# Folding the keys into wq with two half-width column tiles, and 64 bytes ahead of the left-hand tiles

## The chip, the core and the metric

The kernel runs on one core of a Trainium2 chip. The time is the device time of one execution in microseconds; where several runs are shown, their median. Beside the times there is the profile of one execution, with the instructions of every engine, the DMA queues and the TensorE clock that was granted.

## What is computed

Two operators read the same x (2048 tokens of 576 values, float32), and a gate mixes them token by token:

```
g   = sigmoid(sum(x * gate_w))
a   = irfft2(rfft2(x) * (w_r + i w_i))
q   = x @ w_q                       # 32 heads, two halves of 128
s1  = q[..., :128] @ k1.T           # 64 keys;  s2 = q[..., 128:] @ k2.T
e   = 64 * argmax(s1) + argmax(s2)  # one expert of 4096 per token and head
b   = sum over heads of gelu(x . u[e]) * v[e]
out = g * a + (1 - g) * b
```

With one expert per head the softmax over the chosen scores is 1. The table of experts has u and v side by side, so one row is 1,152 float32 values, 4,608 bytes.

## The kernel before, in words

**The keys are folded into w_q.** q itself is never built. For each chunk c of 4 heads (8 chunks) and each block i of the model dimension (four of 128 rows and a last one of 64) the kernel computes M = w_q · k, so that the scores are x · M. That is `build_m` (L442), called 40 times. `load_wq` (L399) brings a block of w_q into a tile of the ring uv, as 8 groups g of 128 columns: 4 heads times two halves. Even g belong to k1, odd g to k2. `kTb` holds the keys, negated, as three blocks of 64 columns: k1, k2, k1. For each g there is one fp32 product: the 128 columns of w_q's group are the stationary operand, and 128 key columns from `half * 64` on are moved. So each product yields 128 columns in PSUM, 64 of the keys wanted and 64 of the other ones. Only the first 64 are read afterwards (`pv()[:, :, :E]` with E = 64). ScalarE copies them as `mh` rounded to the matmul type fp32r (L459), and a remainder `ml` is made: on VectorE in chunk 0 (L468), later by an identity product that subtracts `mh` in PSUM (`less`, L461) and a copy on ScalarE. One call of the fp32 product stands in the profile as two matmuls (passes), each with a weight load of its own.

**Scores.** `scores` (L474) multiplies, for two tiles of 128 tokens at a time, x and its remainder (tiles `xt`) with `mh` and `ml` into PSUM tiles of 1,024 scores, of which there are four. VectorE takes the maximum over each group of 64 (L504); ScalarE makes the signs of the difference to it (L512); VectorE reduces these to an index (L528 to L542), which ScalarE writes out as an expert's number.

**Gathers and their use.** `group` (L631) gathers, for token tiles 0 to 9, one row of 4,608 bytes per token and head from HBM (L638, issued by GpSimd, 128 rows each) into one of the 12 buffers of the ring uv. VectorE forms x · u (L650), ScalarE the gelu, and the v halves are added up in three ways: VectorE alone (L682), ScalarE scaling and VectorE adding (L675, L676), or TensorE with a diagonal matrix (L706). For the token tiles 10 to 15 `quad` (L738) does the same later, with gathers at L745, dots at L754 and TensorE products that use 32 of the array's columns for each of four heads (L766).

**The transform** comes behind the scores: `fold` (L892), then units of `f2`, `f4`, `f5`, `f6`, then `invert` (L1066). `fold` and `f6` use array tiles of 32 columns too. The gathers of `quad` run beside it.

**The order** of the work is a list written out by hand, RANK, one place for each job of the planner (`Plan`, L108), which runs them through a model of the engines and fixes the order on every engine. `mm` (L347) and `on` chain each engine's instructions in that order. A set of products is planned at 1.74 us (`plan("PE", 1.74, ...)`).

**Memory.** Tiles are allocated in pools from the left (pp, sm, gp, then sp, and lb in its place later) and from the right (pad, xp, sa, later la). `pad` is 96 bytes on the right, cleared by a memset at L288. gp holds the 12 buffers of uv and kT, among others; sp holds the tiles `mh`, `ml` and some of `xt`; the tiles with an x at the end of their names (`mhx`, `mlx`) lie in sa, on the right.

The products before:

```
for g in range(8):
    half = g % 2
    mm(
        pv()[:, g, :], wq.ap[:, g, :],
        kTb.ap[:, half * 64 : half * 64 + 128], start=g % 4 == 0, stop=g % 4 == 3, skip_group_check=True)
```

Of the kernel before, what the change touches and what calls it, by code (L numbers as in the profile page):

```python
# [12 lines left out]
F32 = mybir.dt.float32  # L13
# [7 lines left out]
P = 128  # L21
# [7 lines left out]
E = 64  # L29
# [228 lines left out]
def dve(n, psum=False):  # L258
    return 0.07 + n / 960


def act(n):
    return 0.1 + n / 1250
# [15 lines left out]
def tile_kernel(ctx, tc, xn, xT, x5, wqT, wq5, kT, wri, uv, gw, t_kr, t_ff, t_fv, t_tw, t_io, out):  # L279
    nc = tc.nc  # L280
    PS = bass.MemoryType.PSUM

    pools = {}
    pools["pp"] = ctx.enter_context(tc.tile_pool(name="pp", bufs=1))
    pools["sm"] = ctx.enter_context(tc.tile_pool(name="sm", bufs=2))
    pools["gp"] = ctx.enter_context(tc.tile_pool(name="gp", bufs=1))
    pad = ctx.enter_context(tc.tile_pool(name="pad", bufs=1, side="right"))
    nc.vector.memset(pad.tile([P, 24], F32, tag="pad", name="pad"), 0.0)  # L288
    pools["xp"] = ctx.enter_context(tc.tile_pool(name="xp", bufs=1, side="right"))
# [7 lines left out]
    def after(chain, i):  # L297
        if chain in prev:
            tc.add_manual_dep(
                i.ins, prev[chain].ins.name,  # L300
                mybir.DependencyInfo(mybir.DependencyClass.NoSync, mybir.DependencyReason.DATA),
                reason="order of the work")
        prev[chain] = i
# [26 lines left out]
    def buf(tag, shape, dt=F32, view=None):  # L330
        ids[0] += 1
        name = f"{tag if isinstance(tag, str) else tag[0]}_{ids[0]}"

        def make(g, slot):
            p, n = home[g]
            x = pools[p].tile(shape, dt, tag=f"{g}.{slot}", bufs=1, name=name)
            return view(x) if view else x

        return Buf((tag,) if isinstance(tag, str) else tag, make)

    def psum():
        return buf("p2", [P, 2, 512])

    def nd(*k):
        return NUDGE.get(k, 0.0)

    def mm(*args, **kw):  # L347
        after("PE", nc.tensor.matmul(*args, **kw))  # L348
# [8 lines left out]
    def dv(us, at, fn, w, r, **kw):  # L357
        return plan("DVE", us, at, lambda: on("DVE", fn()), w, r, **kw)

    def ac(us, at, fn, w, r, **kw):  # L360
        return plan("ACT", us, at, lambda: on("ACT", fn()), w, r, **kw)
# [30 lines left out]
    kTb = buf("kT", [P, 192])  # L392
# [49 lines left out]
    def build_m(c, i, at, after=()):  # L442
        at = at + nd("b", c, i)
        mh, ml = m_t[c, i] = [
            buf(n + "x" if c % 2 == 0 and i < MX else n, [P, CW], F32R) for n in ("mh", "ml")]
        pm = psum()
        wq = wq_t[c, i]
        pv = lambda: pm.ap.rearrange("p a (g e) -> p (a g) e", e=128)

        def go():  # L450
            for g in range(8):
                half = g % 2
                mm(
                    pv()[:, g, :], wq.ap[:, g, :],
                    kTb.ap[:, half * 64 : half * 64 + 128], start=g % 4 == 0, stop=g % 4 == 3, skip_group_check=True)

        plan("PE", 1.74, at, go, [pm], [wq, kTb], after=after)
        v3 = lambda m: m.ap.rearrange("p (g e) -> p g e", e=E)
        ac(act(512), at + O_MH, lambda: actv(v3(mh), pv()[:, :, :E], AF.Copy, scale=-1.0), [mh], [pm])  # L459
        if c >= LOW_PE:  # L460
            def less():  # L461
                for r in range(2):
                    mm(pv()[:, 4 * r : 4 * r + 4, :E], ident, v3(mh)[:, 4 * r : 4 * r + 4, :], start=False, stop=True, skip_group_check=True)

            plan("PE", 0.25, at + O_LESS, less, [pm], [mh, "ident"])
            ac(act(512), at + O_ML, lambda: actv(v3(ml), pv()[:, :, :E], AF.Copy, scale=-1.0), [ml], [pm])
            return
        dv(dve(512, True), at + O_ML, lambda: stt(v3(ml), pv()[:, :, :E], -1.0, v3(mh).bitcast(F32), op0=ALU.mult, op1=ALU.subtract), [ml], [pm, mh])  # L468
# [964 lines left out]
```

## Time and profile before

| what | value |
|---|---|
| median of 3 runs | 944.68 us (942.21 to 947.41) |
| profiled execution | 953.06 us, span 951.3 us |
| granted TensorE clock, mean | 0.963 |
| products on kT (one of the page's groups) | 640 matmuls, 81.0 us busy |
| gathers: L638 and L745 | 320 and 192, 128 rows each |
| HBM traffic over the span | 362 GB/s |

The profiled execution is one execution and not among the three timed ones. PE is TensorE's matmuls and PEld its weight loads, which run beside them; DVE is VectorE, ACT ScalarE, POOL GpSimd and SP the queue of the plain loads. The tile form 128*32 is the part of the array that a matmul uses, rows times columns; 128*128 is the full array. A matmul's duration in the profile holds its latency, so neighbouring ones overlap; what counts for pace is the step from start to start.

### The profile page before, as it was taken

Reading aid. Unit: us, or ns where it says so; the run is one execution under the profiler, and the core shown is the slowest. Engines: PE = TensorE matmul, PEld = TensorE weight load, DVE = VectorE, ACT = ScalarE, POOL = GpSimd, SP = SyncE. Lnnn points to the kernel's source line nnn. Section 1 sums busy time; section 2 is a strip of 40 time slices with the busy share of each in tenths; the row PEclk is TensorE's granted clock in tenths of the full one; section 3 lists DMA queues with packets and bytes.
Section 4 is the critical chain, followed back from the end, with each engine's and each line's share of the span. In section 5 each row is a group of like instructions: output and inputs, shape, how many; then the busy total and the mean of one; then the engine's idle time right before and its main releaser. Section 6 shows DMA issues by size and latency. Waiting matters only on the chain.

```text
span 951.3 us, 16189 instructions
## 1 busy us (share of the span) xinstructions
PE 862.7 (91%) x5046; PEld 672.4 (71%) x5046; DVE 837.8 (88%) x2043; ACT 654.7 (69%) x2188; POOL 568.5 (60%) x516
## 2 busy tenths in 40 slices
PE   7899999999999999999999995656899879798997
PEld 7688888878877887887788784434566555566775
DVE  3679989999989889899999999899878878897886
ACT  3799996978866877587888889946457352623633
POOL 0237456557557566656657776477777657557762
PEclk9999999999999999999999998878999979899999
DMA  9679998999889989989999999999999999999998
GB/s 315 197 315 365 351 356 330 376 349 380 323 310 387 393 327 359 378 308 345 374 326 405 362 403 373 378 377 391 410 406 408 410 369 360 388 341 380 413 413 355
DMA packets 90901, 345.05 MB, mean 363 GB/s; under 512 B 10112, under 2 KB 10752, under 8 KB 90816
## 3 DMA queue, kind: packets, MB, share of 16 engines
q0 software_dynamic: 73728, 302.02, 82.8%
q1 hardware_dynamic: 17088, 42.01, 12.1%
q8 instruction: 40, 0.66, 0.3%
q14 instruction: 45, 0.37, 0.1%
HBM read 339.27 MB, written 4.72 MB: 362 GB/s over the span
## 4 chain that ended last, share of the span: by engine, by line
DVE 33%; PE 30%; DMA 18%; ACT 9%; issue 8%; POOL 2%; SPq 0%; POOLq 0%; DVEq 0%; ACTq 0%
PE p L348 30%; DMA uv<-uv,ei 12%; DVE uv L650 10%; DVE xn L682 6%; DVE xn L676 4%; DVE mx L504 3%; DMA uv<-uv,eiq 3%; POOL uv L638 2%; ACT sg L512 2%; DVE uv L754 2%; ACT xr L735 2%; ACT fl L931 1%; DVE sq L528 1%; DMA uv<-wqT 1%; DMA uv<-x 1%
## 5 line engine op out<-in xcount | busy, mean ns | idle before, releaser
L638 POOL DMA_INDIRECT uv<-uv,ei x320 | 356.5, 1114 | 264.9 <-issue 58.7
L745 POOL DMA_INDIRECT uv<-uv,eiq x192 | 211.8, 1103 | 101.2 <-PE p L348 53.3
L512 ACT ACTIVATE sg<-p,mx 128x64 bf16<-128x64 f32 x1024 | 233.1, 364 | 45.4 <-DVE mx L504 40.5
L348 PE MATMUL p<-mh,xt 128*128 128x512 f32 x768 | 262.6, 400 | 0.2 <-ACT sg L512 0.2
L650 DVE SCALAR_TENSOR_TENSOR uv<-uv,xn 128x576 f32<-128x576 f32 x320 | 237.7, 755 | 22.4 <-DMA uv<-uv,ei 22.1
L348 PE MATMUL p<-uv,dg 128*32 128x288 f32 (+1 forms) x1072 | 144.0, 429 | 37.0 <-DVE dg L760 23.2
L348 PE MATMUL p<-ml,xt 128*128 128x512 f32 x448 | 176.0, 393 | 0.0
L348 PEld LDWEIGHTS p<-mh,xt 128*128 128x128 f32 x768 | 144.2, 188 | 32.7 <-ACT sg L512 0.6
L754 DVE SCALAR_TENSOR_TENSOR uv<-uv,xr 128x576 f32<-128x576 f32 x192 | 140.9, 753 | 7.0 <-DMA uv<-uv,eiq 6.2
L348 PEld LDWEIGHTS p<-uv,dg 128*32 128x32 f32 (+1 forms) x1072 | 79.8, 136 | 82.1 <-DVE dg L760 27.9
L348 PE MATMUL p<-mhx,xt 128*128 128x512 f32 x384 | 137.0, 403 | 0.3 <-ACT sg L512 0.3
L682 DVE SCALAR_TENSOR_TENSOR xn<-uv,a,xn 128x576 f32<-128x576 f32 x121 | 98.4, 814 | 0.1
L348 PEld LDWEIGHTS p<-ml,xt 128*128 128x128 f32 x448 | 84.2, 188 | 17.8
L348 PE MATMUL p<-kT,uv 128*128 128x128 f32 x640 | 81.0, 283 | 9.2 <-ACT kT L788 5.1
L348 PEld LDWEIGHTS p<-kT,uv 128*128 128x128 f32 x640 | 79.2, 198 | 14.1 <-ACT kT L788 5.1
L676 DVE TENSOR_TENSOR xn<-uv,xn 128x576 f32<-128x576 f32 x113 | 85.5, 757 | 1.0 <-ACT uv L675 0.5
L675 ACT ACTIVATE uv<-uv,a 128x576 f32<-128x576 f32 x113 | 82.9, 780 | 3.9 <-DVE a L663 2.3
L348 PEld LDWEIGHTS p<-mhx,xt 128*128 128x128 f32 x384 | 72.6, 189 | 16.6 <-ACT sg L512 0.7
L504 DVE TENSOR_REDUCE mx<-p 128x16 f32<-128x1024 f32 x64 | 78.1, 1221 | 3.1 <-PE p L348 3.1
L523 ACT ACTIVATE sg<-sg 128x256 bf16<-128x256 bf16 x192 | 79.7, 450 | 0.6
L348 PE MATMUL p<-mlx,xt 128*128 128x512 f32 x192 | 75.6, 394 | 0.0
L735 ACT ACTIVATE xr<-xl 32x576 f32<-32x576 f32 x96 | 65.4, 681 | 3.9 <-DVE uv L650 1.9
(120 smaller groups left out, 1087.8 us busy)
## 6 DMA issues: line engine op xcount, KB each, us to landing
uv<-wqT SPq DMA_DIRECT2D x32, 512.0 KB, 6.9
uv<-uv,ei POOLq DMA_INDIRECT x320, 7.2
w<-wri SPq DMA_DIRECT2D x16, 289.0 KB, 6.9
out<-xn SPq DMA_DIRECT2D x16, 288.0 KB, 6.2
uv<-uv,eiq POOLq DMA_INDIRECT x192, 7.9
xn<-xn SPq DMA_DIRECT2D x10, 288.0 KB, 6.2
tw<-t_tw SPq DMA_DIRECT2D x9, 256.0 KB, 6.6
uv<-xT SPq DMA_DIRECT2D x8, 256.0 KB, 6.4
```

The source lines that it names most:

```text
L348: after("PE", nc.tensor.matmul(*args, **kw))
L504: dv(dve(1024, True), at + O_MAX + nd("m", c, tp), lambda: nc.vector.tensor_reduce(mv.ap[:, 2 * tp : 2 * tp + 2, :], ps.ap.rearrange("p a ...
L512: on("ACT", actv(sg.ap[:, j, g, :], ps.ap[:, j, g * E : g * E + E], AF.Sign, bias=mv.ap[:, 2 * tp + j, g : g + 1], scale=-1.0))
L523: ac(act(256), at + O_ADD, lambda b=b: actv(s2()[:, :, b * Q : b * Q + Q], s2()[:, :, b * Q : b * Q + Q], AF.Copy, bias=b / 4), [sg], [])
L638: on("POOL", nc.gpsimd.indirect_dma_start(out=g.ap.rearrange("p a d -> p (a d)"), out_offset=None, in_=uv, in_offset=bass.IndirectOffsetOn ...
L650: dv(0.68, at + O_DOT + nd("d", t, c), lambda k=k, g=rows[k], xk=xk: stt(g.ap[:, 0, :], g.ap[:, 0, :], 1.0, xk.ap, op0=ALU.mult, op1=ALU.m ...
L675: ac(act_by(576), at + O_SCALE + nd("v", t, c), lambda v=v, s=s: actv(v(), v(), AF.Copy, scale=s()), [(rows[k], 1)], [a])
L676: dv(dve(576), at + O_SUM + nd("v", t, c), lambda v=v: vt(y.ap, v(), y.ap, ALU.add), [y], [(rows[k], 1)])
L682: dv(0.73, at + O_SUM + nd("v", t, c), lambda v=v, s=s: stt(y.ap, v(), s(), y.ap, op0=ALU.mult, op1=ALU.add), [y], [(rows[k], 1), a])
L735: ac(0.69, at + 0.6 * j, lambda j=j, q=q: actv(xr[t][j].ap[QB * q : QB * q + QB, :], x.ap[QB * j : QB * j + QB, :], AF.Copy), [(xr[t][j], ...
L745: on("POOL", nc.gpsimd.indirect_dma_start(out=g.ap.rearrange("p a d -> p (a d)"), out_offset=None, in_=uv, in_offset=bass.IndirectOffsetOn ...
L754: dv(0.68, at + O_QDOT + nd("d", t, c), lambda j=j: stt(rows[j].ap[:, 0, :], rows[j].ap[:, 0, :], 1.0, xr[t][j].ap, op0=ALU.mult, op1=ALU. ...
```

## The change

Each product over the full array becomes two: one for each half of the 128 stationary columns, with the result in PSUM partitions 0 to 63 and 64 to 127. Both move only the 64 key columns that are read later. So a set is 16 calls instead of 8, and the unused 64 columns of each group are no longer written. A tile of 64 bytes per partition is allocated first in pool gp and cleared by a memset on VectorE, so all tiles of gp, and those of sp and lb behind it, lie 64 bytes further on. RANK and all planned durations are kept, and so is the order.

```diff
     pools["gp"] = ctx.enter_context(tc.tile_pool(name="gp", bufs=1))
+    nc.vector.memset(pools["gp"].tile([P, 16], F32, tag="edge", name="edge"), 0.0)
     pad = ctx.enter_context(tc.tile_pool(name="pad", bufs=1, side="right"))
...
             for g in range(8):
                 half = g % 2
-                mm(
-                    pv()[:, g, :], wq.ap[:, g, :],
-                    kTb.ap[:, half * 64 : half * 64 + 128], start=g % 4 == 0, stop=g % 4 == 3, skip_group_check=True)
+                for d in (0, 64):
+                    mm(
+                        pv()[d : d + 64, g, :E], wq.ap[:, g, d : d + 64],
+                        kTb.ap[:, half * E : half * E + E], start=g % 4 == 0, stop=g % 4 == 3, skip_group_check=True)
```

## The prediction

> **What bounds the kernel now.** I read the page first, then the table of the two long stretches, then the chain of waits and the table of waits, and last the timeline round the products that change.
>
> ```profile
> PE 862.7 (91%) x5046; PEld 672.4 (71%) x5046; DVE 837.8 (88%) x2043; ACT 654.7 (69%) x2188; POOL 568.5 (60%) x516
> ...
> PE   7899999999999999999999995656899879798997
> ...
> DVE  3679989999989889899999999899878878897886
> ...
> DVE 33%; PE 30%; DMA 18%; ACT 9%; issue 8%; POOL 2%; SPq 0%; POOLq 0%; DVEq 0%; ACTq 0%
> ```
>
> ```profile
> 60.00:580.00 520.00, 511.29 (x2476) 419.62 (x2475) 495.04 (x1125) 423.03 (x1582) 317.83 (x285) 1.00 0.94 354
> 600.00:951.00 351.00, 290.19 (x2250) 201.30 (x2240) 294.18 (x815) 174.55 (x435) 228.09 (x207) 0.92 0.99 387
> ```
>
> The columns of the table are length, then busy time of PE, PEld, DVE, ACT and POOL, the granted clock, the DMA share and GB/s. There are two regimes. From 60 to 580 us (the scores) TensorE is busy 98% of the time and VectorE 95%, with the DMA engines at 0.94: nearly balanced, and no engine has room. From 600 us on TensorE falls to 83% and the DMA engines stand at 0.99: that stretch is paced by the gathers. The change works on TensorE in the first regime alone, so the question is how much of TensorE's time there lies on the path.
>
> ```profile
> 36.36 37.53 PE p L348 x182
> ...
> 212.81 42.53 PE p L348 x217
> ...
> 320.31 18.90 PE p L348 x96
> ```
>
> ```profile
> 36.36:73.89 37.53, 6.78 (x48) 0.95 0.67 251
> 212.81:255.34 42.53, 7.62 (x64) 1.00 0.92 344
> 320.31:339.21 18.90, 4.10 (x32) 1.00 0.91 344
> ```
>
> The chain runs through TensorE in three long pieces before 580 us, 99 us together. The second fence is the busy time of the products on kT in just these pieces: 48, 64 and 32 matmuls, so 3, 4 and 2 of the 40 sets of products (a set is 16 matmuls). The other 31 sets are beside the chain. Between the pieces the chain is VectorE, ScalarE and gathers.
>
> ```profile
> L504 DVE TENSOR_REDUCE mx<-p 128x16 f32<-128x1024 f32 x64 | 78.1, 1221 | 3.1 <-PE p L348 3.1
> ...
> PE p L348 <- ACT sg L512: 0.7, 3, 0.3
> ...
> DVE uv L650 <- DMA uv<-uv,ei: 16.9, 30, 1.4
> ...
> POOL uv L638 <- PE p L348: 20.0, 24, 3.4
> ```
>
> The first row is of the groups, the other three of the waits from 60 to 580 us (total, times, longest). VectorE's maximum over the scores waited for TensorE 3.1 us in the whole run. TensorE in turn waited 0.7 us for its PSUM tiles. What VectorE does wait for is gathered rows (16.9 us), and some gathers wait for a buffer that TensorE frees (20.0 us in 24 waits, 0.8 each).
>
> **The products now.** A set is 8 fp32 products, each two passes, each pass a weight load of 128 columns and a matmul over 128 key columns.
>
> ```profile
> 109.20 1.95 PE L348 MATMUL p<-kT,uv 128*128 128x128 f32 x16
> 110.90 0.48 PE L348 MATMUL p<-mh,xt 128*128 128x512 f32 x1
> 111.22 0.40 PE L348 MATMUL p<-ml,xt 128*128 128x512 f32 x1
> 111.45 0.39 PE L348 MATMUL p<-mh,xt 128*128 128x512 f32 x1
> ...
> 115.60 3.73 PE L348 MATMUL p<-kT,uv 128*128 128x128 f32 x32
> 119.09 0.48 PE L348 MATMUL p<-mh,xt 128*128 128x512 f32 x1
> 119.41 0.40 PE L348 MATMUL p<-ml,xt 128*128 128x512 f32 x1
> ```
>
> The first score matmul behind a block starts early but lasts longer, as its load lies bare; so I count to the second one and take off one score step (111.45 − 111.22 = 0.23). A lone set costs 111.22 − 109.20 − 0.23 = 1.79 us, 0.112 a pass. Two in a row cost 119.41 − 115.60 − 0.23 = 3.58.
>
> **The products after.** Each becomes two, on array columns 0-63 and 64-127, each moving 64 key columns: 32 matmuls and 32 loads a set, 640 more of each in all. No row of before shows a 128*64 tile. The nearest are the 128*32 tiles of the transform.
>
> ```profile
> 753.66 0.38 PE L348 MATMUL p<-tw,t 128*128 128x256 f32 x1
> ...
> 753.97 0.64 PE L348 MATMUL p<-tw,t 128*32 128x128 f32 x16
> ...
> 753.97 0.38 PEld L348 LDWEIGHTS p<-tw,t 128*32 128x32 f32 x16 [0.33 <-issue]
> ...
> 755.16 0.43 PE L348 MATMUL p<-uv,dg 128*32 128x288 f32 x4
> 755.52 0.51 PE L348 MATMUL p<-t,tw 128*128 128x289 f32 x1
> ```
>
> ```profile
> L348 PEld LDWEIGHTS p<-uv,dg x1072: 106/110/338, 144.1 to 946.7; 128*32 128x32 f32 x129, 128*128 128x128 f32 x50
> ...
> L348 PE MATMUL p<-tw,t x384: 272/297/634, 715.0 to 863.4; 128*32 128x128 f32 x128, 128*128 128x256 f32 x64
> ...
> L348 PEld LDWEIGHTS p<-kT,uv x640: 186/192/338, 5.1 to 507.3; 128*128 128x128 f32 x160
> ```
>
> Sixteen matmuls of 128 columns in 128*32 tiles take 0.64 from first start to last end; without the last one's own 0.27 that is 0.37 between starts. The 16 of a set, same columns, take 1.95 − 0.27 = 1.68. So four tiles run side by side: 4 rounds of about 0.11 instead of 16 steps. I take the same for two tiles of 64. A round is then half of 0.112, as stream and load are both halved: 0.056. A set is 16 rounds, 0.90.
>
> The change of tile form is not free. Into small tiles: the full-array matmul of 753.66 streams 256 columns (0.22 at 0.112 per 128), so is fed by 753.88, and the next starts at 753.97: 0.09 of nothing, then a bare load (192 − 110 ns for 96 columns more, so 0.05 for 64). Out of them: the last four of 288 columns start at 755.16 and stream about 0.25, to 755.42 with their stagger; the next starts at 755.52 and lasts 0.51 where the four last 0.41: 0.10 of nothing and 0.10 of bare load. Together 0.34 a block. The Trainium skill, "TensorEngine Tiling (Array Packing)", section "Tiling Modes", speaks against the change here: it says that switching the tiling mode drains the array, and gives no time; the trace agrees with 0.09 and 0.10 us.
>
> A lone set: 0.34 + 0.90 = 1.24 instead of 1.79, saves 0.55. Two in a row: 0.34 + 1.80 = 2.14 instead of 3.58, saves 1.44. One set, behind a long wait, runs at a lower clock:
>
> ```profile
> 36.36 3.05 PE L348 MATMUL p<-kT,uv 128*128 128x128 f32 x16 [3.55 <-DMA uv<-wqT]
> 39.07 0.77 PE L348 MATMUL p<-mhx,xt 128*128 128x512 f32 x1
> ```
>
> 39.07 − 36.36 = 2.71 where the warm one takes 110.90 − 109.20 = 1.70: it saves 0.55 × 1.6 = 0.88.
>
> **On the chain.** First piece: the cold set and one pair, 0.88 + 1.44 = 2.3. Second: two lone sets and a pair, 1.10 + 1.44 = 2.5. Third: two lone sets, 1.1. So 5.9 us is the most that the chain can give if all else in it stays as long. It will give less, for each piece ends where something else is nearly as late.
>
> ```profile
> 73.91 1.23 DVE L504 TENSOR_REDUCE mx<-p 128x16 f32<-128x1024 f32 x1 [0.21 <-PE p L348]
> ```
>
> The first piece ends in a maximum that waited 0.21 us; earlier in that piece VectorE waited for TensorE more, but all its waits for it are 3.1. The cold set's 0.88 shortens those waits in full, the pair behind it only the last short ones: I take 1.3 of 2.3. The second piece ends in a gather that waits for a freed buffer; such a wait is 0.8 on average, behind which the next releaser is due: 0.8 of 2.5. The third ends in ScalarE's copy of a set's own result, and goes on to VectorE, which is 95% busy: 0.8 of 1.1. Sum 2.9. The five sets before 36 us end in the 3.55 wait for a load of wq, which covers them, and the sets beside the chain make TensorE wait for PSUM instead.
>
> **The rest of the change.** The 64 bytes need one memset on VectorE.
>
> ```profile
> 0.82 0.08 DVE L288 MEMSET pad<- 128x24 f32 x1 [0.82 <-PEq L1422]
> 9.07 0.69 DVE L420 TENSOR_TENSOR xt<-uv,xt 128x512 fp32r<-128x512 f32 x1 [8.18 <-ACT xt L419]
> ```
>
> The like of it took 0.08 us, and VectorE then idles 8 us: nothing. All left-hand tiles of gp and behind it move by 64 bytes.
>
> ```profile
> L348 PE MATMUL p<-mh,xt 128*128 128x512 f32 x768 | 262.6, 400 | 0.2 <-ACT sg L512 0.2
> ...
> L348 PE MATMUL p<-mhx,xt 128*128 128x512 f32 x384 | 137.0, 403 | 0.3 <-ACT sg L512 0.3
> ```
>
> Tile mhx lies on the right at other offsets than mh on the left, and the same matmul takes 403 and 400 ns: for the engines I take zero, with that 1% either way as its bound; for gathers see the third rival. Semaphores, queues and the order of all engines stay: no instruction passes another.
>
> **Sum.** The profiled execution took 953.06 us (span 951.3), 0.9% over the median of the three runs shown, 944.68. 953.06 − 2.9 = 950.2; the same 2.9 off the median gives **941.8 us**.
>
> **Rivals.**
> *The halves run one behind the other (slower).* If two 128*64 tiles do not overlap, in loading, streaming or for want of instructions (64 a set in 0.9 us, 14 ns each; the 32 of the transform above came at 0.37/32 = 12), a set is 32 passes of 0.056 = 1.79 again, and each block pays 0.34. From 36.36 to 505.77 us the timeline has 31 blocks, a pair counted once: 10.5 us on an engine that has 8.7 idle from 60 to 580. At least the 7 blocks of the chain count (2.4), at most all: midway 6.5, 951.2 us. It decides as soon as a round of two passes is over 1.45/16 = 0.09. Against it: the fourfold overlap above. For it: each of those loads is of 32 columns, so four make no more than one full load, while here the loads must run at twice the rate shown. The skill's same section says that tiles load and multiply in parallel; by it this rival falls.
> *Nothing comes through.* VectorE's 495 us of work from 60 to 580 stay, and it waits for TensorE hardly at all; then TensorE only waits more, for PSUM: 944.7. For it: the 3.1 us.
> *The 64 bytes speed up the gathers.*
>
> ```profile
> q0 software_dynamic: 73728, 302.02, 82.8%
> q1 hardware_dynamic: 17088, 42.01, 12.1%
> ```
>
> The tiles before gp end 192 bytes past a multiple of 256 (8,640, by the program's allocation), and a gather's row is 4,608 = 18 × 256, as kT's is 3 × 256: all twelve buffers start at 192, and afterwards at 0. Off the boundary a row touches 19 stretches of 256 bytes, on it 18. If a transfer's time goes by these, it falls by 1/19, and the stretch behind 600 us, which is at the gathers' pace, gains 351 × 0.828 / 19 = 15.3: with the 2.9, 926.5 us. The Trainium skill, "DMA: Bandwidth & Descriptors", section "How a descriptor splits into AXI transactions", has such a rule: an unaligned start also pays for the bytes from the boundary on, by which I estimate 144 instead of 150 beats, or 11.5 us. Against it: q0 costs 0.828 × 16 × 951.3 / 302.02 = 41.7 us per MB on one engine, q1 43.8 with smaller packets and tiles on other offsets, so no surcharge shows; but no transfer to a 256-byte start is there to compare.
>
> **How the numbers follow.** The forecast (0 to 5.9 off, centre 2.9) has 0.44, nothing 0.19, the serial halves 0.20, the gathers 0.12, and 0.05 is for a fixed order that fits its new times worse. A measurement of this kernel tells about 0.5% from no change, 4.7 us: under 940.0 is faster, over 949.4 slower. Faster: the gathers and some 40% of the forecast, whose upper part is over 4.7 with the noise, 0.30. Slower: most of the serial case and the misfit, 0.21. Same: 0.49. The range goes from 934, part-way to the gathers' case, to 951, the middle of the serial case.
>
> **What would show it.** Right: products as 128*64, 64 columns, x1280, a lone block about 1.2 us to the next score step; TensorE's busy time from 60 to 580 down, its waits for ScalarE's signs (0.7) up to ten or more; VectorE's idle time nearly as before. Serial halves: blocks of 2.1 us and TensorE busy throughout. Gathers: fewer us per MB on q0, and a shorter stretch behind 600 us. I am wrong in kind if VectorE's wait for gathered rows (16.9) falls by more than half, or rises.

## The result, and the profile after

On one chip, 12 runs of each, the median went from 948.75 to 943.09 us; the ratio is 0.9947 with an interval of [0.9927, 0.9966]: faster by 0.3 to 0.7%. The two profiled executions differ by more, 953.06 and 941.53 us, because the one of before lies just above all of its own timed runs (942.21 to 952.64) and the one of after near the lower end of its own (941.09 to 946.62). So stages of the two are compared here with care, and single operations freely. In this document a median is of all runs of a kernel, and a ratio leaves out the slow runs, those over 1.5% above the fastest of the same kernel.

The page of after, the rows that stand in the prediction for before:

```profile
PE 841.5 (90%) x5686; PEld 642.6 (68%) x5686; DVE 836.0 (89%) x2044; ACT 653.6 (70%) x2188; POOL 564.9 (60%) x516
...
PE   7899999999999999998999995665899879798998
...
DVE 35%; PE 29%; DMA 14%; ACT 11%; issue 9%; POOL 2%; SPq 0%; DVEq 0%; POOLq 0%; ACTq 0%
```

TensorE has 640 more matmuls and 21 us less work. VectorE and ScalarE do the same work as before. The table by stretch (length; busy time of PE, PEld, DVE, ACT, POOL; granted clock; DMA share; GB/s) of after:

```profile
60.00:580.00 520.00, 497.00 (x2985) 396.76 (x2983) 498.07 (x1137) 426.86 (x1605) 319.26 (x289) 0.99 0.95 359
```

TensorE is busy 497.0 instead of 511.3 us in these 520, and VectorE, at 498.1, is now the busier of the two. The same 520 us hold a little more of the program than before: the last maximum over the scores, which ends the score stage, starts 7 us earlier. Before and after:

```profile
580.96 1.22 DVE L504 TENSOR_REDUCE mx<-p 128x16 f32<-128x1024 f32 x1
...
573.80 1.22 DVE L506 TENSOR_REDUCE mx<-p 128x16 f32<-128x1024 f32 x1
```

The timeline of TensorE in after shows a lone set and, further on, two in a row:

```profile
106.46 1.15 PE L349 MATMUL p<-kT,uv 128*64 128x64 f32 x32
107.54 0.50 PE L349 MATMUL p<-mh,xt 128*128 128x512 f32 x1
107.88 0.39 PE L349 MATMUL p<-ml,xt 128*128 128x512 f32 x1
...
113.66 2.08 PE L349 MATMUL p<-kT,uv 128*64 128x64 f32 x64
115.67 0.50 PE L349 MATMUL p<-mh,xt 128*128 128x512 f32 x1
116.01 0.39 PE L349 MATMUL p<-ml,xt 128*128 128x512 f32 x1
```

By the prediction's own rule (to the second score matmul, less one score step of 0.23) a lone set takes 107.88 − 106.46 − 0.23 = 1.19 us, forecast 1.24 and 1.79 before; a pair takes 116.01 − 113.66 − 0.23 = 2.12, forecast 2.14 and 3.58 before. Behind 60 us there are 32 sets, 26 lone and 3 pairs: TensorE is spared 26 × 0.60 + 3 × 1.46 = 20.0 us. So the products do what was worked out for them. Whether the 5 us come from them is another matter.

The waits of TensorE in after from 60 to 580 us (total, times, longest):

```profile
PE p L349 <- ACT mh L461: 8.5, 6, 3.0
PE p L349 <- ACT dg L706: 4.8, 6, 2.2
PE p L349 <- ACT mhx L461: 2.6, 3, 1.1
PE p L349 <- ACT sg L514: 2.1, 4, 0.7
```

The same table of before starts with this row:

```profile
PE p L348 <- ACT mh L459: 4.6, 4, 2.3
```

So TensorE waited most for the copies that ScalarE makes of the sets' own results (`mh`) already before; for the signs `sg` it waited 0.7. Now it waits longer for these copies.

One thing in the trace of after stands in no forecast. Between two products on kT there are stretches of score matmuls alone. One of them is the same in all kernels, from a matmul on `mlx` to the `mlx` that comes 78 score matmuls later, without a gap. Its first and its last row, in the timeline of before:

```profile
299.37 0.39 PE L348 MATMUL p<-mlx,xt 128*128 128x512 f32 x1
...
317.37 0.39 PE L348 MATMUL p<-mlx,xt 128*128 128x512 f32 x1
```

and of after:

```profile
295.17 0.39 PE L349 MATMUL p<-mlx,xt 128*128 128x512 f32 x1
...
312.88 0.39 PE L349 MATMUL p<-mlx,xt 128*128 128x512 f32 x1
```

The durations are equal, 0.39, but the steps are not: 18.00 / 78 = 230.8 ns before, 17.71 / 78 = 227.1 ns after. A matmul's row includes the time in which the next one already streams; what it costs is the distance from start to start. Over all back-to-back score matmuls behind 60 us (some 1,500 steps in each trace) the mean is 230.8 ns before and 227.8 after. There are 1,792 score matmuls, so this alone is 1,792 × 3.0 ns = 5.4 us of TensorE's work, spread evenly over the scores. The change does nothing to these instructions. It only moves tiles by 64 bytes.

### The profile page after: what moved, and what is told of

Read it like the earlier page. It is cut to its first block, busy times and chain, and to the rows that moved or that the text cites. A ratio compares the mean times of both kernels' runs of the same rounds, so it can differ in the third digit from the quotient of the medians.

```text
span 939.8 us, 17470 instructions
## 1 busy us (share of the span) xinstructions
PE 841.5 (90%) x5686; PEld 642.6 (68%) x5686; DVE 836.0 (89%) x2044; ACT 653.6 (70%) x2188; POOL 564.9 (60%) x516
## 4 chain that ended last, share of the span: by engine, by line
DVE 35%; PE 29%; DMA 14%; ACT 11%; issue 9%; POOL 2%; SPq 0%; DVEq 0%; POOLq 0%; ACTq 0%
PE p L349 29%; DMA uv<-uv,ei 11%; DVE uv L652 11%; DVE xn L684 6%; DVE xn L678 4%; DVE mx L506 4%; ACT sg L514 3%; ACT xr L737 2%; DMA uv<-xT 2%; ACT uv L677 1%; POOL uv L640 1%; DVE uv L756 1%; ACT fl L933 1%; DVE sq L530 1%; DVE im L541 1%
## 5 line engine op out<-in xcount | busy, mean ns | idle before, releaser
L349 PE MATMUL p<-uv,dg 128*32 128x288 f32 (+1 forms) x1072 | 146.5, 430 | 36.2 <-DVE dg L762 22.4
L349 PEld LDWEIGHTS p<-kT,uv 128*64 128x64 f32 x1280 | 43.4, 145 | 25.8 <-issue 8.8
L349 PE MATMUL p<-kT,uv 128*64 128x64 f32 x1280 | 48.9, 233 | 12.8 <-ACT kT L790 4.9
## 6 DMA issues: line engine op xcount, KB each, us to landing
out<-xn SPq DMA_DIRECT2D x16, 288.0 KB, 5.7
xn<-xn SPq DMA_DIRECT2D x10, 288.0 KB, 6.4
```

## Experiments

After the result there were two theories. **The tiles:** part of the 20 us that the column tiles save on TensorE comes through, as forecast. **The 64 bytes:** the tiles bring nothing, and the memory placement brings it all, either through the score step, or through the gathers, as the third rival had it. The first four kernels ran on one chip, 5 rounds each, against 945.98 us for the kernel before.

**The column tiles without the 64 bytes.** The changed kernel without this line:

```
-    nc.vector.memset(pools["gp"].tile([P, 16], F32, tag="edge", name="edge"), 0.0)
```

> The column tiles alone, without the 64 bytes. Theory A (the shorter sets of products on TensorE make the gain, the 64 bytes nothing): ratio to before 0.993 to 0.997, as the whole change; a lone set 1.19 us to the next full step. Theory B (the 64 bytes speed up the gathers, the products are hidden behind VectorE): 0.998 to 1.002.

Measured: 947.75 us, ratio 1.000 [0.9974, 1.0025]. The stretch of 78 steps in its timeline:

```profile
297.67 0.40 PE L348 MATMUL p<-mlx,xt 128*128 128x512 f32 x1
...
315.69 0.39 PE L348 MATMUL p<-mlx,xt 128*128 128x512 f32 x1
```

18.02 / 78 = 231.0 ns, as before. The sets are as short as in after (1.19 us), and nothing of it is seen in the time. Its waits from 60 to 580 us say where TensorE spends the time instead:

```profile
PE p L348 <- ACT mh L460: 10.1, 8, 3.1
PE p L348 <- ACT sg L513: 6.1, 9, 2.3
PE p L348 <- ACT dg L705: 3.5, 5, 1.5
```

From 60 us to 578, just before the last maximum of the scores starts, the two tables by stretch give for before and for this kernel:

```profile
60.00:578.00 518.00, 510.28 (x2473) 419.08 (x2472) 493.06 (x1122) 421.03 (x1575) 316.90 (x284) 1.00 0.94 354
...
60.00:578.00 518.00, 495.69 (x2969) 391.99 (x2967) 490.94 (x1119) 418.87 (x1571) 318.42 (x284) 0.99 0.94 353
```

TensorE is idle 7.7 us in before and 22.3 here: 14.6 of the 20.0 saved come back as waits. Another part comes back as clock, told below. That last maximum starts at 581.1 here and at 581.0 in the trace of before. These are single executions, and this one, 952.02 us, is the longest of its kernel's twelve.

**The 64 bytes without the column tiles.** The kernel before with that line added.

> The 64 bytes alone, with the old products. Theory A: ratio 0.998 to 1.002, us per MB on the gathers' queue as before. Theory B: 0.993 to 0.997, and the gathers' queue 2% or more cheaper per MB.

Measured: 941.86 us, ratio 0.996 [0.9939, 0.9981]. The stretch:

```profile
292.92 0.39 PE L349 MATMUL p<-mlx,xt 128*128 128x512 f32 x1
...
310.63 0.39 PE L349 MATMUL p<-mlx,xt 128*128 128x512 f32 x1
```

17.71 / 78 = 227.1 ns. One memset, and the kernel with the old products gains 3.8 us (1.8 to 5.8), about as much as the whole change. The last maximum starts at 572.2. The tiles alone have it at 581.1 on this chip, but in a long execution; the next two kernels, which have the old step of 230.8 ns and executions of 944.2 and 943.5 us, have it at 577.0. So, as far as single executions tell, some 5 us of the difference go with the step. Beside this kernel the whole change keeps its longer waits: to 3 us before its last maximum TensorE is idle 6.7 us here and 19.6 in after, and that maximum comes no earlier there (573.8). The queues of this kernel's page:

```profile
q0 software_dynamic: 73728, 302.02, 83.6%
q1 hardware_dynamic: 17088, 42.01, 12.2%
```

The gathers (q0) take 0.836 × 940.0 = 785.8 us of the sixteen engines; in before it is 0.828 × 951.3 = 787.7, in the tiles alone 792.5, in after 784.7. A drop by 1/19 would have been 41 us. The gathers do not get cheaper by anything like it.

**The full array, moving 64 key columns only.** The old products, without the columns that nobody reads:

```
-                    pv()[:, g, :], wq.ap[:, g, :],
-                    kTb.ap[:, half * 64 : half * 64 + 128], start=g % 4 == 0, stop=g % 4 == 3, skip_group_check=True)
+                    pv()[:, g, :E], wq.ap[:, g, :],
+                    kTb.ap[:, half * E : half * E + E], start=g % 4 == 0, stop=g % 4 == 3, skip_group_check=True)
```

> Full-array products as before, but each moves only the 64 key columns that are read; no column tiles, no 64 bytes. Theory A with the weight load as the bound of a pass: a pass stays near 0.11 us, a lone set 1.75 to 1.8, ratio 0.998 to 1.002. Rival (the moved columns were the bound): a pass 0.056, a lone set about 0.95 with no change of tile form to pay, ratio 0.990 to 0.995, better than the column tiles.

Measured: 947.13 us, ratio 1.0019 [1.0000, 1.0038]. A lone set in its timeline:

```profile
108.66 1.89 PE L348 MATMUL p<-kT,uv 128*128 128x64 f32 x16
110.36 0.48 PE L348 MATMUL p<-mh,xt 128*128 128x512 f32 x1
110.67 0.40 PE L348 MATMUL p<-ml,xt 128*128 128x512 f32 x1
```

110.67 − 108.66 − 0.23 = 1.78 us, for half the columns moved, as before (1.79). Each pass still takes 0.11, so moving half the columns saves nothing. The next experiment halves the loaded columns, and there a pass takes half: it is the load of 128 columns that sets the pace here. The Trainium skill, "TensorE: Matmul & The Clock Gate", section "LDWEIGHTS (loading the stationary operand)", says that a load goes by its columns, P / 1.2 ns, by which I estimate 107 ns for 128 and 53 for 64; the trace agrees with 0.11 here and, within 10%, with 0.058 in the next experiment.

**The halves one behind the other.** The column tiles without the 64 bytes, but all products of columns 0-63 first; against the changed kernel:

```
+            for d in (0, 64):
+                for g in range(8):
...
-            for g in range(8):
-                for d in (0, 64):
```

> The same column tiles, but all eight products of the lower half of the columns first, then the eight of the upper half; no 64 bytes. If matmuls start in the order of the program, the halves cannot overlap: a lone set 32 x 0.056 + 0.34 = 2.1 us, 0.3 more than before, ratio 1.003 to 1.011. This prices the rival of the prediction. If each half of the array runs ahead by itself: a set 1.2 us and a ratio of 0.993 to 0.997.

Measured: 947.25 us, ratio 1.0021 [1.0002, 1.0040].

```profile
109.68 1.90 PE L348 MATMUL p<-kT,uv 128*64 128x64 f32 x32
111.51 0.50 PE L348 MATMUL p<-mh,xt 128*128 128x512 f32 x1
111.84 0.40 PE L348 MATMUL p<-ml,xt 128*128 128x512 f32 x1
```

111.84 − 109.68 − 0.23 = 1.93 us. Within a half the passes start 58 to 59 ns apart, so one behind the other. Only in the middle of a set, where the halves meet, do three rounds of two start together, 4 to 6 ns apart. Two tiles run side by side, then, only where products on them stand close together in the program. This is the forecast's serial rival made real, and it measures 2.0 us over before (0.2 to 3.8), where the rival had 6.5. How much of the 2.0 is the serial order is not shown: the kernel of the last experiment, with sets as long as before, measures 1.8 over it.

So the products can take 1.19, 1.78 or 1.93 us a set, and without the 64 bytes the time is the same within 0.4%. Two questions were left: what in the 64 bytes brings it, and why TensorE's saving does not. Four kernels ran on another chip, on which the kernel before takes 991.9 us.

**The right-hand pad 160 bytes instead of 96, no 64 bytes on the left, old products.** SBUF is filled from both ends. In before the left-hand tiles of the scores lie at 64 modulo 256 bytes, the right-hand ones at 128. The 64 bytes bring the left ones to 128. This edit brings the right ones to 64, so both sides agree again, while the gathers' buffers stay at 192 as in before:

```
-    nc.vector.memset(pad.tile([P, 24], F32, tag="pad", name="pad"), 0.0)
+    nc.vector.memset(pad.tile([P, 40], F32, tag="pad", name="pad"), 0.0)
```

> Old products, nothing on the left; instead the memset tile on the right grows from 96 to 160 bytes, so all right-hand tiles move by 64 bytes and the gather buffers stay at 192 past a multiple of 256. Theory C (new: what counts is the distance of TensorE's moving and stationary tiles, 64 bytes off a multiple of 128 before, none after): the mean step of the score matmuls falls from 230.8 to about 228 ns and the ratio is 0.994 to 0.998, as with the 64 bytes on the left. Theory B (gathers that start at a multiple of 256): 0.998 to 1.002, since no gather buffer moves.

Measured: 987.06 us, ratio 0.9937 [0.9889, 0.9984].

```profile
305.37 0.40 PE L348 MATMUL p<-mlx,xt 128*128 128x512 f32 x1
...
323.09 0.39 PE L348 MATMUL p<-mlx,xt 128*128 128x512 f32 x1
```

17.72 / 78 = 227.2 ns, with gathers untouched. The short step comes from the two sides agreeing, wherever they agree. The time fell as well, but the next kernel shows that this proves little.

**128 and 192 bytes on the left.** `edge` as a tile of 32 and of 48 float32; the left-hand tiles then lie at 192 and at 0, the right-hand ones at 128 still.

> Old products, 128 bytes ahead of the left-hand tiles instead of 64. Theory C: left and right are again 64 off, so the step stays near 231 ns and the ratio is 0.998 to 1.002. A theory by which any shift helps (a luckier placement, or another timing of the start): 0.994 to 0.998.

> Old products, 192 bytes ahead of the left-hand tiles: gather buffers at 128 past a multiple of 256, left- and right-hand tiles of TensorE 128 apart modulo 256. Theory C with a period of 128 bytes: step about 228 ns, ratio 0.994 to 0.998. Theory C with a period of 256: step 231, ratio near 1.000. Theory B: 0.998 to 1.002, no gather buffer starts at a multiple of 256.

Measured: 987.09 us, 0.9955 [0.9902, 1.0009], and 991.78 us, 0.9997 [0.995, 1.0045]. Neither interval excludes no change, and the first one's median is that of the pad of 160 bytes. So on this chip the times do not tell equal sides from another shift; the steps do. The mean steps over the scores are 229.8 and 230.6 ns, nearer to before (230.8) than to the kernels whose sides agree (227.8 to 228.0).

**Each set made twice.** The whole change, with `for _ in range(2):` around a set's products: the second pass through them repeats the work, to load TensorE.

> The whole change, with every set of products made twice (the second time with the same result): a lone set 0.90 us longer, some 31 us more work for TensorE from 36 us on. If the sets are hidden behind ScalarE's copies and VectorE: ratio to the old kernel below 1.002, under 6 us more than the change. If TensorE's time there is on the path: 20 to 31 us more than the change, ratio 1.015 to 1.03.

Measured: 1010.77 us, ratio 1.0229 [1.0174, 1.0285]: 22.7 us more than before (17 to 28). A lone set in its timeline:

```profile
117.69 2.09 PE L349 MATMUL p<-kT,uv 128*64 128x64 f32 x64
119.70 0.50 PE L349 MATMUL p<-mh,xt 128*128 128x512 f32 x1
120.04 0.39 PE L349 MATMUL p<-ml,xt 128*128 128x512 f32 x1
```

120.04 − 117.69 − 0.23 = 2.12, so 0.93 more than in after, 30 us for the 32 sets behind 60 us. But the edit adds more than that, for many of its sets have gaps in them ("issue": TensorE waits for nothing that the profile shows), as here:

```profile
235.29 1.50 PE L349 MATMUL p<-kT,uv 128*64 128x64 f32 x44
237.01 0.37 PE L349 MATMUL p<-kT,uv 128*64 128x64 f32 x5 [0.22 <-issue]
237.74 0.34 PE L349 MATMUL p<-kT,uv 128*64 128x64 f32 x3 [0.36 <-issue]
```

From the first product of a block to the next other matmul, all blocks behind 60 us take 90.2 us here and 55.7 in the kernel with the pad of 160 bytes, which has the old products, the short step and ran on the same chip. That is 34.5 us more, and the medians of the two differ by 23.7. TensorE's work is on the path, then: most of what is added there is paid for. What the tiles take away is not paid back. That VectorE and ScalarE stand right behind TensorE would explain this, but it is argued, not shown, and it does not say why the shorter steps of the 64 bytes are paid back for the most part.

**Where the rest of the saving goes.** Only the sum of waits was clear so far. The timeline of TensorE in after, behind its longest wait:

```profile
433.01 0.39 PE L349 MATMUL p<-mh,xt 128*128 128x512 f32 x1
436.44 0.80 PE L349 MATMUL p<-mh,ident 128*128 128x256 f32 x2 [3.04 <-ACT mh L461]
437.03 0.63 PE L349 MATMUL p<-mh,xt 128*128 128x512 f32 x1
437.46 0.63 PE L349 MATMUL p<-ml,xt 128*128 128x512 f32 x1
437.89 0.63 PE L349 MATMUL p<-mh,xt 128*128 128x512 f32 x1
```

and its table by stretch:

```profile
138.70:142.10 3.40, 3.40 (x9) 2.82 (x10) 3.37 (x9) 3.28 (x16) 0.68 (x1) 0.50 0.59 184
435.60:442.50 6.90, 6.06 (x16) 4.99 (x17) 6.90 (x18) 4.33 (x16) 5.50 (x5) 0.51 0.97 353
```

The score steps are 0.43 instead of 0.23 us (437.89 − 437.46), and the granted clock is 0.51 for 6.9 us; behind a wait of 1.47 us at 138.7 it is 0.50 for 3.4 us more. So 10.3 us ran at half pace, 5 us lost. In the tiles alone it is 3.4 us twice (at 288.0 and 373.3, behind waits of 1.50 and 2.32), 3.4 lost. With the 14.6 of waits that is 18.0 of the 20.0 us saved. In before, in the 64 bytes alone, in the full array with 64 columns and in the halves in turn the clock never falls between 40 and 579 us. That sum fits, but it doesn't separate cause from effect: a clock drop makes TensorE slower where it had time to spare, and may cost nothing there. Before has waits of 2.27 and 1.54 us without a drop, and the tiles alone have one of 3.08. And on the other chips drops inside the scores are seen with the old products too (once in the kernel with the pad of 160 bytes, at 299.3; four times in the one with 192 bytes on the left). The Trainium skill, "TensorE: Matmul & The Clock Gate", section "What's actually happening", says that the clock is halved after an idle window of some 3.4 us, in windows that run by themselves; the lengths of 3.4 and 6.8 us agree, but here waits of 1.5 to 3.0 us were enough.

**The four corners once more.** To size the tiles' share beside equal sides, four kernels ran together on a third chip (before: 993.35 us): the 64 bytes alone, the pad of 160 alone, the column tiles with the pad of 160, and the whole change. The edits are those above.

> The 64 bytes in front of the left-hand tiles alone, products as before; beside the next three kernels on one chip. Theory A (the gain comes from left-hand and right-hand tiles standing at the same offset modulo 256 bytes): score step 227.8 ns instead of 230.8, 1,792 steps, so 5.4 us of TensorE's work less and 4 to 5 us off the time, ratio 0.995 to 0.996. Theory B (the gain is the gathers'): the same time, with the score step as it may be and fewer us per MB on the gathers' queue.

> The right-hand pad of 96 bytes made 160, nothing in front of the left-hand tiles, products as before: the two sides agree again, now at offset 64, and the gathers' buffers stay where they were. Theory A: as the kernel with the 64 bytes, 0.995 to 0.996, step 227.9 ns. Theory B: no change, 1.000.

> The column tiles with the pad of 160 bytes in place of the 64 bytes on the left. Theory A: as the whole change, ratio within 0.2% of it, step 227.9 ns in spite of gathers at their old offset. Theory B: as the column tiles alone, 1.000. For the share of the column tiles: if they add nothing once the sides agree, this ratio equals that of the pad alone; if the forecast's 2.9 us come through, it lies 0.3% under it.

> The whole change again, on the same chip as the three others. Theory A with tiles that add nothing: equal to the 64 bytes alone, 0.995 to 0.996. With the forecast's 2.9 us for the tiles: 0.992 to 0.993. Idle time of TensorE in the scores 21 us again where the kernels with the old products have about 9, with a stretch or two of half clock.

Measured: 986.8 us, 1.0089 [1.0012, 1.0167]; 989.39 us, 0.9991 [0.9921, 1.0061]; 992.67 us, 1.005 [1.0001, 1.0099]; 987.72 us, 1.0023 [0.9961, 1.0085]. As times these settle nothing. The runs of a kernel spread over 1.4 to 3.5% on this chip. By the medians three of them are 0.4 to 0.7% faster and the tiles with the pad 0.1%; by the ratios none is shown to be faster. The expectation in times was missed, for one theory as for the other. The step was met in all four: 227.8, 227.9, 228.0 and 227.9 ns, so also with the tiles and the pad together, and with the gathers at their old offset. The expected idle time came in part: from 60 to 578 us TensorE is idle 27.2 us in the whole change and 12.7 in the 64 bytes alone, but both have two stretches of half clock in the scores, so these are not the tiles' own. The sets of the two kernels with tiles also show some gaps of the kind seen above, some 2.2 us in each; on the first chip they show none.

**Which placement matters.** In the traces each score matmul can be put down by the place of the tile that it moves and of the one that is loaded for the next matmul meanwhile (x is the stationary operand; both operands lie on either side). A row names the side of the moved tile; the side of x follows from the token tile, which I count in the program's order: 0 to 7 lie on the right, 8 to 15 on the left. Offsets are modulo 256 bytes; times are mean steps in ns behind 60 us, with the number of steps:

```
moved tile   next weights    before          after
left         left            64 / 64   229.1 (552)   128 / 128  227.9 (530)
left         right           64 / 128  233.3 (521)   128 / 128  227.8 (518)
right        left           128 / 64   230.6 (237)   128 / 128  228.2 (228)
right        right          128 / 128  229.4 (205)   128 / 128  227.4 (203)
```

Within one trace of one kernel, the step is 4 ns longer where the next weights lie 64 bytes further on than the moved tile, and 1 to 1.5 longer where they lie 64 bytes back. The 64 bytes make all four the same. The kernel with 128 bytes on the left tests this, as its sides are 64 bytes apart the other way round: there left to right takes 229.8 and right to left 233.1 ns, so the two change places. With 192 bytes, 128 apart both ways, they take 232.2 and 232.1. One thing does not fit: right to right stands at 128 / 128 in both kernels of the table and still falls from 229.4 to 227.4. So the pair is not all of it, and what else shortens these steps is not shown. The Trainium skill, "TensorE: Matmul & The Clock Gate", section "Step-by-step: what each phase is for", says that loading the next weights takes no read bandwidth from the running matmul, as each has a read port of its own; these rows differ from that by 0.5 to 2%.

## Why the prediction was right, and where not

The number was right, 941.8 forecast and 943.09 measured, in the range; the change in it, 2.9 us forecast, came out as 5.0 (0.53%, 0.34 to 0.73). The reason for it was wrong, and the agreement is luck: a gain forecast for the products was absent, and one put at zero took its place. By its steps:

- **What bounds the kernel.** Right: nearly balanced. Some 34 us more in TensorE's sets cost some 24; taking off 20 in the tiles alone gives 0 (at most 2.5).
- **A set after the change, 1.24 us, and a pair, 2.14.** Right: 1.19 and 2.12. The overlap of two tiles of 64 could be read off the transform's four tiles of 32, and its two gaps of 0.09 and 0.10 with their bare loads were a good price for the switch.
- **On the chain 2.9 (1.3 + 0.8 + 0.8).** This step failed. Each of the three was "what the next releaser leaves", and it left nothing that the runs can show: the tiles alone are at 1.000 [0.9974, 1.0025], and in the whole change beside the 64 bytes alone, measured at another time, they give 0.1% (0.9947 against 0.996, each within 0.2%). Of the waits of TensorE the working took up those for the signs, 0.7, and left out the longest, 4.6 for the sets' own copies, and there the saving went. The chain shows how long the latest path is, not how far the next one is behind; that VectorE, 95% busy, is that next path all along is my reading and not tested. The rival "nothing comes through" was right for the tiles.
- **The 64 bytes, zero for the engines.** This step failed as well, and it covered for the other. The value was 1.3% of the score step, in favour, a little outside the bound of 1% either way: 5.4 us on 1,792 matmuls, beside a gain of 3.8 for the 64 bytes alone. The bound was never turned into time: 1% of 1,792 × 230.8 ns is 4.1 us, more than the whole forecast. The rows of `mh` and `mhx`, 400 and 403 ns, couldn't show it: they are durations, not steps, and each is a mean over next weights from both sides. The steps by pairs stood in the trace of before: 233.3 against 229.1.
- **The gathers gain from a start at 256.** Fell: q0 takes the same time per MB at either offset, and the pad of 160 bytes has the short step without moving them. (The 11.5 us there come to 11.6 by their own figures.)
- **The serial halves, 951.2.** The tiles do overlap, in the order that the change has. Where the order is turned round they hardly do, and that measures 2.0, not 6.5: a set is then 1.93 us, only 0.14 over before where 0.34 was taken, as three rounds overlap where the halves meet, and 32 passes come at 54 ns on average, not 56.
- **What would show it.** TensorE's idle time from 60 to 578 us rose as said, from 7.7 to 21.0 us, but behind the copies of `mh` (8.5) rather than the signs (2.1). VectorE's idle time hardly fell (25.0 to 21.9 in the 520 us), and its wait for gathered rows fell from 16.9 to 12.5, by about a quarter. All of these come out so whether or not the shorter sets bring any time: no sign was named that could tell the tiles from what the 64 bytes do to TensorE.

What stays open: how the 64 bytes' 5.4 us of shorter steps become the time that is seen, and whether all of it comes by them, since the tiles' 20 us did not, the pad of 160 bytes showed a gain on one chip (0.9937, with a kernel of longer steps beside it at 0.9955) and on the third (0.9991, with 0.7% either way) showed none; whether the tiles have a share of a tenth of a per cent or two, and whether the clock drops or VectorE and ScalarE alone keep it away. A planned order with the sets' new length, 1.19 instead of 1.74, wasn't tried.

## What to carry to other kernels

In this kernel one engine is 98% busy and the next 95%; work added to the first was paid for in most part, and 20 us taken off in 32 sets were not paid back. So a chain gives an upper bound of the gain and not its size: ask what the engine waits for next, its own results' copies included. Measure back-to-back work from start to start and by the place of its operands, as a change that shifts memory can move thousands of small steps. When an edit has two parts, forecast each for itself; here the gain hoped of the products came with the 64 bytes.

## What the runs showed of the hardware

- The step of a 128x512 score matmul goes by the offset modulo 256 bytes of the moved tile against the tile that is loaded for the next matmul: 227.4 to 229.4 ns where they agree (shorter when all tiles of the kernel agree), 233.3 with the weights 64 bytes further on, 230.6 with them 64 bytes back.
- An fp32 pass over the full array takes 0.11 us with 128 moved columns and with 64: the load sets it.
- Two tiles of 64 columns run side by side if products on them alternate (1.19 us a set), and nearly all one behind the other if the products of one tile follow each other (1.93).
- Waits of 1.47 to 3.04 us were followed by 3.4 or 6.9 us at half clock in some cases, and waits of 1.54, 2.27 and 3.08 in others were not.
